# Attention and two gated layers on one core: batch 0's transposed q copied by either engine, its left-over tokens transposed after the first scores, another seed of the planner

## The chip, the cores and the metric

The kernel runs on one core of a Trainium2 chip. The metric is the device time of one launch in microseconds (us), and the time quoted for a kernel is the median of its runs. The core's engines are TensorE (PE in the profile; PEld is its loading of weights), VectorE (DVE), ScalarE (ACT), GpSimd (POOL) and SyncE (SP), which here issues nearly all DMAs. Each engine works through its own list of instructions in order.

## The reference

Three layers follow each other, all in float32 (the scales of the inputs are left out).

```python
# attention over 32 memory slots: q, k, v are (4, 8, 576, 64), phi is (4, 8, 576, 32)
a = softmax(phi, axis=2)                       # over the 576 tokens
k_m, v_m = einsum('bhsm,bhsd->bhmd', a, k), einsum('bhsm,bhsd->bhmd', a, v)
attn = softmax(q @ k_m.T / 8, axis=-1)         # over the 32 slots
x = (attn @ v_m) as (2304, 512)
# first layer, 512 -> 1536 -> 512
xn = x / sqrt(mean(x * x) + 1e-6) * rms_g
x = (silu(xn @ w_gate) * (xn @ w_val)) @ w_out
# second layer, 512 -> 2048 -> 512
h = x @ w_in
g = where(h >= 1, h, where(h <= -1, 0, (h + 1) ** 2 / 4))
out = g @ w_out2
```

## The kernel before, in words

**The order is made by a planner.** The program is written as some hundred streams (Python generators). A stream yields the engine that its next step needs with the planner's guess of its duration (`yield "A", 0.6` is 0.6 us of ScalarE), then emits the step. The class `Agenda` holds the streams and picks at each turn the one that can start first, by priority where they tie. A yield such as `"VAhi", (0.45, 0.68)` lets the planner pick the engine (V for VectorE, A for ScalarE, G for GpSimd) that would be done first. `"flag"` waits until another stream has called `mark`, `"take"` and `"give"` count buffers. The order in which steps are emitted is the order in which every engine runs them. Line 54 holds `SEED, WOBBLE`: each planned duration is multiplied by a random factor within 3% of 1 (in `run`), drawn from that seed, so another seed gives another order of the whole program, and with it other choices of engine.

**Attention, per batch b.** `soft` takes the maximum of phi over the tokens (folds on line 516, TensorE steps of lines 534 and 545), subtracts it (line 553, VectorE) and exponentiates (line 521, ScalarE). The tile is phi0 to phi3. `memory` sums phi-weighted k and v on TensorE (line 606, tile kvps), adds the sums of the weights (line 625, which wait for tile s1, made on GpSimd for batches 1 to 3), divides on VectorE (lines 635 to 652, tiles r, kd, vs), transposes (lines 660 and 663, tile kT) and copies the memory keys to kmT (line 669, ScalarE). `spread_v` (line 687) makes vbd from vs on VectorE or GpSimd.

**Scores.** `pair` handles 256 tokens of one batch; there are two pairs for each batch, and two further ones for the left-over 64 tokens of two batches each. A pair transposes its q on TensorE in two halves (line 772, tile qps), and `copy_q` copies each half to qT with ScalarE (line 758). Then `scores` multiplies qT with kmT (line 723, tile sc). The softmax over slots follows: maximum (line 791), difference (797), exponential (806), sum (810), its inverse (812, 813) and the product with it (815), then a transpose (823), its copy (827), the product with vbd (844, tile xp), squares (835), the scaling on GpSimd (856 to 862), a last transpose (870, tile ATp) and the split into a high and a low part (881, 883: Ah and Al, for batches 2 and 3 in the tile late).

**Left-over q.** `rest_q(b)` transposes the left-over 64 tokens of q (line 708, tile qrps) once q of the batch is there, and copies them with ScalarE (line 712, tile qr). Its score step is on line 734. The tile q0 is free for another batch when all three of its readers (two pairs and `rest_q`) have emitted their transposes.

**Weights and the first layer.** While this goes on, the weights of the first layer are loaded as raw 64-bit words (line 326) and turned into floats (`convert`, lines 339 to 362, on three engines; line 346 is the GpSimd form of the step on line 344). `vw` multiplies them with the batch's memory values on TensorE (line 934, tile vwps), ScalarE and VectorE split the result (952, 954). `gv` makes gate and value (line 984, tiles gps and vps; gps0_0_1 is batch 0, chunk 0, second half); `gate`, `splits` and `out1` (line 1079, tile ops) follow, then the second layer (`quads` line 1423, `outs` line 1546).

**Heat.** Until kmT3 is there, `heat` fills gaps that the planner sees on TensorE with matmuls of zeros (line 586).

Of the kernel before, what the change touches and what calls it, by code (L numbers as in the profile page):

```python
# [13 lines left out]
AF = mybir.ActivationFunctionType  # L14
# [36 lines left out]
OVER = {"V": 0.085, "A": 0.1}  # L51
FETCH = (256, 63, 80.0, 6.1, 3.6, 80)
TICK = 3.413
SEED, WOBBLE = 4, 0.06
WARM = 1.38
P_SOFT, P_PAIR, P_CONV, P_VW, P_GV, P_OUT1, P_W2, P_F2 = 0, 100, 800, 102, 850, 900, 3000, 4000
P_W = 4004
# [172 lines left out]
def tile_attn_moe(tc, q, k, v, phi, w_gate, w_val, w_out1, rms_g, w_in2, w_out2, out):  # L230
# [10 lines left out]
    nc = tc.nc  # L241
# [37 lines left out]
    def bank(tag, name):  # L279

        early = BANKS.get(tag + "0") if "attention" not in agenda.flags else None
        z = yield "pick", early or BANKS[tag]
        return psum.tile([P, 512], F32, tag=f"b{z}", name=name), ("bank", z)
# [23 lines left out]
    add, mark = agenda.add, agenda.set  # L307
# [388 lines left out]
    def used_q(b):  # L696
        q_left[b] -= 1
        if q_left[b] == 0:
            yield "give", "q"

    def rest_q(b):
        yield "flag", ("q", b)
        yield "take", "qr"
        qp, q_bank = yield from bank("q", f"qrps{b}")
        yield "P8", 0.43
        qv = qp.rearrange("p (c n) -> p c n", c=4)[0:D]
        for c in range(4):
            nc.tensor.transpose(qv[:, c, :], q_t[b][:, c, J - 1, :], ident)
        yield from used_q(b)
        yield "A", 0.6  # L710
        t = qr_t[b] = st.tile([P, 4, P], F32, tag="qr", name=f"qr{b}", bufs=BUFS["qr"])[0:D]
        nc.scalar.activation(out=t, in_=qv, func=AF.Copy)
        yield "give", q_bank
        mark(("qr", b))

    def scores(pr, qT, scv, w):
        if pr[0] < B:
            for i in range(2):
                yield "Ps32", 0.5
                for c in range(2 * i, 2 * i + 2):  # L720
                    for g in range(2):
                        for k in range(2):
                            nc.tensor.matmul(  # L723
                                out=scv[HP * k : HP * k + HP, 4 * g + c], lhsT=qT[:, c, g, k],
                                rhs=kmT_t[pr[0]][:, 4 * g + c].rearrange("p j m -> p (j m)"),
                                start=True, stop=True, skip_group_check=True,
                            )
            yield "give", "qT"
            return
        yield "Ps64", 1.0  # L730
        for c in range(4):
            for g in range(2):
                for k, bb in enumerate(RESTS[pr[1]]):
                    nc.tensor.matmul(
                        out=scv[HP * k : HP * k + HP, 4 * g + c], lhsT=qr_t[bb][:, c, HP * g : HP * g + HP],
                        rhs=kmT_t[bb][0:D, 4 * g + c, 0], start=True, stop=True, skip_group_check=True,
                    )
        for _ in RESTS[pr[1]]:
            yield "give", "qr"
# [6 lines left out]
    def pair(n):  # L746
        pr = pairs[n]
        b, jj = pr
# [5 lines left out]
        qT = None  # L754

        def copy_q(i, qv, q_bank):
            yield "A", 0.6
            nc.scalar.activation(out=qT[:, :, :, i], in_=qv, func=AF.Copy)
            yield "give", q_bank
            mark(("qT", pr, i))  # L760

        if b < B:
            yield "flag", ("q", b)
            yield "take", "qT"
            qT = st.tile([P, 4, 2, 2, HP], F32, tag="qT", name=f"qT_{name}", bufs=BUFS["qT"])
            for i in range(2):
                qp, q_bank = yield from bank("q", f"qps_{name}_{i}")
                yield "P8", 0.43
                qv = qp.rearrange("p (c g n) -> p c g n", c=4, g=2)
                j = 4 * jj + 2 * i  # L770
                for c in range(4):
                    nc.tensor.transpose(  # L772
                        qv[:, c].rearrange("p g n -> p (g n)"), q_t[b][:, c, j : j + 2].rearrange("p j d -> p (j d)"), ident
                    )
                add(pri, copy_q(i, qv, q_bank))
            yield from used_q(b)
        else:
            for bb, _ in per_batch(pr):
                yield "flag", ("qr", bb)
        for bb, _ in per_batch(pr):  # L780
            yield "flag", ("km", bb)
        if b < B:
            for i in range(2):
                yield "flag", ("qT", pr, i)
        sc, s_bank = yield from bank("s", f"sc_{name}")
        sc = sc[:, 0 : NB * M]
        yield from scores(pr, qT, sc.rearrange("p (h n) -> p h n", h=H), w)
        yield "take", "e"
        yield "V", 0.11 + 0.56 * w
        mx = st.tile([P, H, I], F32, tag="mx", name=f"mx_{name}", bufs=BUFS["e"])  # L790
        nc.vector.tensor_reduce(
            out=mx.rearrange("p h j -> p (h j)"), in_=sc.rearrange("p (n m) -> p n m", m=M),
# [5 lines left out]
            out=et, in0=sc.rearrange("p (h j m) -> p j h m", h=H, j=I),  # L798
# [15 lines left out]
        eng = yield "GVe", (0.2 + 0.9 * w, 0.12 + 0.57 * w)  # L814
        (nc.vector if eng == "V" else nc.gpsimd).tensor_tensor(
            out=e, in0=e, in1=sm.unsqueeze(2).to_broadcast([P, NB, M]), op=ALU.mult
# [22 lines left out]
        for i in range(I):  # L839
            xp, x_bank = yield from bank("x", f"xp_{name}_{i}")  # L840
            yield f"P{8 * len(per_batch(pr))}", 0.86
            for g in range(2):
                for bb, rows in per_batch(pr):
                    nc.tensor.matmul(  # L844
                        out=xp[rows, 256 * g : 256 * g + 256],
# [6 lines left out]
        for i in range(I):  # L852
# [4 lines left out]
            out=y, in0=ss, scalar1=1.0 / DM, scalar2=1e-6, op0=ALU.mult, op1=ALU.add  # L857
# [5 lines left out]
            out=ev, in0=ev, in1=y.unsqueeze(2).to_broadcast([P, I, HM]), op=ALU.mult  # L863
# [345 lines left out]
    for n in range(len(pairs)):  # L1209
        add(P_PAIR + n, pair(n))  # L1210
        if pairs[n][0] < B and pairs[n][1] == 1:
            add(P_PAIR + n, rest_q(pairs[n][0]))
# [456 lines left out]
```

## Time and profile before

| what | us |
|---|---|
| median of the runs shown (3) | 773.75 |
| the runs | 773.43, 773.75, 1912.09 |
| the profiled execution, its own time | 773.81 |
| its span | 772.0 |
| TensorE busy in it, zeros included | 759.0 |
| VectorE, ScalarE, GpSimd busy in it | 621.6, 462.7, 61.1 |

The span runs from the first to the last instruction of the profiled execution, and 1.8 us of its time lie outside the span. The prediction works in times of the span's start (so 21.00 us is 21.00 us into the span). A row of the timeline is: start, duration, engine, line, operation, what it writes and reads, how many such instructions are merged in the row, and in brackets how long the engine sat idle before it and what ended that. Matmuls are pipelined, so that the durations in a row with x1 overlap those of its neighbours. TensorE runs a plain f32 multiplication as two passes, which is why the trace counts 32 where the order prints x16.

### The profile page before, as it was taken

The numbers are of one execution on the slowest core, as the hardware profiler recorded it, in microseconds if no ns is written. First come the engines' busy times: TensorE is split into PE (matmuls) and PEld (weight loads), VectorE is DVE, ScalarE is ACT, GpSimd is POOL, SyncE is SP. The second block draws the span as 40 slices with busy tenths as digits, with TensorE's granted clock in tenths as the row PEclk, the third lists the DMA queues.
The fourth block names the chain that finished last, engine by engine and source line by source line (L and its number), as shares of the span: only waits on it lengthen the run. The fifth ranks groups of instructions, "written<-read, shape, count | busy, mean of one in ns | idle before, by whom it ended". The sixth has DMA issues, their size and how long they took to land.

```text
span 772.0 us, 17234 instructions
## 1 busy us (share of the span) xinstructions
PE 759.0 (98%) x6383; PEld 700.6 (91%) x6383; DVE 621.6 (81%) x1257; ACT 462.7 (60%) x959; POOL 61.1 (8%) x84
## 2 busy tenths in 40 slices
PE   8899999999999999999999999999999999999997
PEld 4678888889999888988899999999999999999997
DVE  5798889998877787756789889997789895589963
ACT  2688887755556555645566656564467463565552
POOL 1556610000001000000000000000000000000000
PEclk9999999999999999999999999999999999999999
DMA  9995535788779775599647999779888878757866
GB/s 343 377 385 160 199 111 188 258 275 270 253 237 305 251 248 187 205 324 324 208 168 219 326 305 305 252 249 318 293 251 262 296 241 258 254 182 251 270 217 209
DMA packets 113371, 197.49 MB, mean 256 GB/s; under 512 B 10372, under 2 KB 41096, under 8 KB 113288
## 3 DMA queue, kind: packets, MB, share of 16 engines
q1 hardware_dynamic: 112368, 194.88, 75.4%
q10 hardware_dynamic: 920, 1.51, 0.5%
q8 instruction: 51, 0.84, 0.4%
q14 instruction: 32, 0.26, 0.1%
HBM read 151.26 MB, written 45.09 MB: 254 GB/s over the span
## 4 chain that ended last, share of the span: by engine, by line
PE 92%; DVE 3%; DMA 2%; ACT 1%; issue 1%; ACTq 0%; SPq 0%; DVEq 0%
PE ops L1079 18%; PE acc_b L1546 17%; PE qb L1423 12%; PE gps L984 10%; PE vps L984 10%; PE qc L1423 6%; PE acc_c L1546 6%; PE qa L1423 3%; PE vwps L934 3%; PE xp L844 2%; DMA kv<-in_k_dram 1%; PE kvps L606 1%; PE sc L723 1%; PE qps L772 1%; DMA x1B<-x_d 1%
## 5 line engine op out<-in xcount | busy, mean ns | idle before, releaser
L1079 PE MATMUL ops<-ab,wo1h 128*128 128x512 f32 (+1 forms) x480 | 137.2, 371 | 0.5 <-ACT xs L1093 0.5
L1423 PE MATMUL qb<-xop,wr 128*128 128x384 f32 x576 | 111.7, 337 | 0.0
L1423 PEld LDWEIGHTS qb<-xop,wr 128*128 128x128 f32 x576 | 100.3, 187 | 0.9 <-DVE xop L1298 0.5
L1079 PEld LDWEIGHTS ops<-ab,wo1h 128*128 128x128 f32 x480 | 84.7, 189 | 15.8 <-issue 2.9
L1079 PE MATMUL ops<-ab,wo1l 128*128 128x512 f32 (+1 forms) x240 | 88.4, 368 | 0.0
L1546 PE MATMUL acc_b<-wor,gg_A 128*128 128x256 f32 x648 | 80.8, 280 | 1.0 <-ACT gg_A L1494 0.8
L1546 PEld LDWEIGHTS acc_b<-wor,gg_A 128*128 128x128 f32 x648 | 79.3, 188 | 1.3 <-ACT gg_A L1494 1.0
L1385 ACT ACTIVATE u<-qb 128x384 f32<-128x384 f32 x72 | 35.2, 489 | 49.7 <-PE qb L1423 49.1
L1423 PE MATMUL qc<-xop,wr 128*128 128x384 f32 x288 | 58.3, 337 | 0.0
L1546 PE MATMUL acc_c<-wor,gg_S 128*128 128x256 f32 x432 | 53.0, 279 | 0.0
L1079 PEld LDWEIGHTS ops<-ab,wo1l 128*128 128x128 f32 x240 | 45.2, 188 | 7.9
L1546 PEld LDWEIGHTS acc_c<-wor,gg_S 128*128 128x128 f32 x432 | 52.2, 188 | 0.0
L1546 PE MATMUL acc_b<-wor,gg_S 128*128 128x256 f32 x432 | 51.7, 279 | 0.0
L1546 PEld LDWEIGHTS acc_b<-wor,gg_S 128*128 128x128 f32 x432 | 51.3, 188 | 0.0
L1423 PEld LDWEIGHTS qc<-xop,wr 128*128 128x128 f32 x288 | 50.9, 187 | 0.0
L344 ACT ACTIVATE raw<-raw 128x512 uint32<-128x512 uint32 x68 | 45.3, 673 | 0.0
L1016 ACT ACTIVATE kvth<-gps 128x64 f32<-128x64 f32 (+2 forms) x101 | 28.9, 305 | 18.8 <-PE gps L984 18.5
L984 PE MATMUL gps<-late,vwh 128*128 128x288 f32 x192 | 39.6, 294 | 0.0
L984 PE MATMUL vps<-late,vwh 128*128 128x288 f32 x192 | 39.6, 294 | 0.0
L1050 ACT ACTIVATE ab<-kvth 128x512 fp32r<-128x512 f32 (+1 forms) x40 | 22.7, 566 | 26.1 <-PE ops L1079 26.1
L954 DVE TENSOR_TENSOR vwl<-vwps,vwh 128x512 fp32r<-128x512 f32 x48 | 32.3, 685 | 7.2 <-ACT vwh L952 6.9
L1494 ACT ACTIVATE gg_S<-gs 128x384 fp32r<-128x384 f32 x52 | 26.8, 522 | 17.5 <-PE acc_b L1546 8.5
(188 smaller groups left out, 1730.1 us busy)
## 6 DMA issues: line engine op xcount, KB each, us to landing
wr<-win_d SPq DMA_DIRECT2D x168, 256.0 KB, 4.0
wor<-wout_d SPq DMA_DIRECT2D x168, 256.0 KB, 3.3
raw<-in_moe_w_out_dram SPq DMA_DIRECT2D x28, 512.0 KB, 4.9
win_d<-wins SPq DMA_DIRECT2D x56, 256.0 KB, 2.8
wout_d<-wouts SPq DMA_DIRECT2D x56, 256.0 KB, 2.9
raw<-in_moe_w_in_dram SPq DMA_DIRECT2D x16, 512.0 KB, 4.9
raw<-in_moe_w_gate_dram SPq DMA_DIRECT2D x12, 512.0 KB, 4.8
raw<-in_moe_w_val_dram SPq DMA_DIRECT2D x12, 512.0 KB, 5.7
```

The lines of the kernel that those rows point to most:

```text
L344: nc.scalar.activation(out=low, in_=low, func=AF.Copy, scale=LOW_SCALE, bias=LOW_BIAS)
L844: nc.tensor.matmul(out=xp[rows, 256 * g : 256 * g + 256], lhsT=aT[:, i, g, rows], rhs=vbd_t[bb][:, g].rearrange("p h d -> p (h d)"), start ...
L934: nc.tensor.matmul(out=vps[g][0][32 * c : 32 * c + 32, 2 * P * x : 2 * P * x + 2 * P], lhsT=vT[n // NF1 * 2 + x][hs, c, :], rhs=t[hs, c].r ...
L954: nc.vector.tensor_tensor(out=lv, in0=vps[g][0], in1=hv.bitcast(F32), op=ALU.subtract)
L984: nc.tensor.matmul(out=p[:, 0:HB], lhsT=wt[:, g, i, :], rhs=at[b][:, g, c], start=(g == 0 and y == 0), stop=(g == 1 and y == 2),)
L1016: nc.scalar.activation(out=t, in_=g[:, c], func=AF.Silu)
L1050: nc.scalar.activation(out=ah, in_=src, func=AF.Copy)
L1079: nc.tensor.matmul(out=p[:, 0:n], lhsT=wt[:, fc, d], rhs=at, start=(fc == 0 and x == 0), stop=(fc == NF1 - 1 and x == 2),)
L1385: nc.scalar.activation(out=u, in_=src, func=AF.Copy)
L1423: nc.tensor.matmul(out=bank, lhsT=wt[:, kc, :], rhs=xt[:, kc, :], start=(start and kc == 0 and i == 0), stop=(kc == 1 and i == 2), skip_gr ...
L1494: nc.scalar.activation(out=t[:, 0], in_=src, func=AF.Copy)
L1546: nc.tensor.matmul(out=acc[x + "001"[t]][:, t % 2], lhsT=g[:, gi, P * t : P * t + P], rhs=w[:, wi], start=((o, t) in FIRST and q == 0 and ...
```

## The change

Three edits. The copies of batch 0's transposed q may go to ScalarE or to VectorE, as the planner picks (0.60 and 0.62 us in its book); those of the other batches stay on ScalarE. The left-over tokens of q of batch 0 are transposed only once the scores of the first pair (0, 0) have been emitted. The seed is 17 instead of 4.

```diff
-SEED, WOBBLE = 4, 0.06
+SEED, WOBBLE = 17, 0.06
...
     def rest_q(b):
+        if b == 0:
+            yield "flag", ("sc", (0, 0))
         yield "flag", ("q", b)
         yield "take", "qr"
...
         def copy_q(i, qv, q_bank):
-            yield "A", 0.6
-            nc.scalar.activation(out=qT[:, :, :, i], in_=qv, func=AF.Copy)
+            if b == 0:
+                eng = yield "AVq", (0.6, 0.62)
+            else:
+                yield "A", 0.6
+                eng = "A"
+            if eng == "A":
+                nc.scalar.activation(out=qT[:, :, :, i], in_=qv, func=AF.Copy)
+            else:
+                nc.vector.tensor_copy(out=qT[:, :, :, i], in_=qv)
             yield "give", q_bank
             mark(("qT", pr, i))
...
         yield from scores(pr, qT, sc.rearrange("p (h n) -> p h n", h=H), w)
+        mark(("sc", pr))
         yield "take", "e"
```

**TensorE at the first scores.** qps_0_1_1 is the last of batch 0's four transposed pieces of q, qrps0 its left-over tokens, sc_0_0 and sc_0_1 the scores of its two pairs. Before:

```order
L772 MATMUL qps_0_1_0_291<-ident_85,q0_176 128x128 x4
L772 MATMUL qps_0_1_1_324<-ident_85,q0_176 128x128 x4
L708 MATMUL qrps0_292<-ident_85,q0_176 64x128 x4
L723 MATMUL sc_0_0_338<-kmT0_104,qT_0_0_288 64x64 x16
L586 LDWEIGHTS zeros_115
L586 MATMUL heat_123<-zeros_115 128x512
```

The same place of the changed kernel:

```order
L781 MATMUL qps_0_1_0_292<-ident_85,q0_177 128x128 x4
L781 MATMUL qps_0_1_1_323<-ident_85,q0_177 128x128 x4
L725 MATMUL sc_0_0_333<-kmT0_104,qT_0_0_289 64x64 x16
L725 MATMUL sc_0_1_353<-kmT0_104,qT_0_1_291 64x64 x16
L710 MATMUL qrps0_362<-ident_85,q0_177 64x128 x4
L586 LDWEIGHTS zeros_115
L586 MATMUL heat_123<-zeros_115 128x512
```

The left-over tokens moved behind both scores. The zeros between the scores (four matmuls before, then one behind sc_0_1) now stand together behind the left-over tokens, five of them, ahead of kvps1.

**ScalarE at the copies of q.** qT_0_1 is the transposed q of pair (0, 1), phi1 the exponential of batch 1. Before:

```order
L758 ACTIVATE qT_0_0_288<-qps_0_0_1_305 128x8x64
L758 ACTIVATE qT_0_1_290<-qps_0_1_0_291 128x8x64
L521 ACTIVATE phi1_165<-phi1_165 128x1152
L712 ACTIVATE qr0_357<-qrps0_292 64x512
L758 ACTIVATE qT_0_1_290<-qps_0_1_1_324 128x8x64
L806 ACTIVATE e_0_0_370<-e_0_0_370 128x512
```

Now:

```order
L765 ACTIVATE qT_0_0_289<-qps_0_0_1_304 128x8x64
L765 ACTIVATE qT_0_1_291<-qps_0_1_0_292 128x8x64
L521 ACTIVATE phi1_166<-phi1_166 128x1152
L714 ACTIVATE qr0_388<-qrps0_362 64x512
L816 ACTIVATE e_0_0_379<-e_0_0_379 128x512
L816 ACTIVATE e_0_1_394<-e_0_1_394 128x512
```

One of batch 0's four copies left ScalarE, the second half of qT_0_1. On VectorE it stands between vT0 and the first maximum, as the only new row there (`L767 COPY`).

**TensorE at batch 3's memory.** kT3 holds the memory keys and values of batch 3 transposed, s13 the sums of its weights, vwps1 chunk 1 of the weights times the memory values, gps0_0_1 a gate product. Before:

```order
L625 MATMUL kvps3_1_1017<-consts_67,s13_1014 128x1
L772 MATMUL qps_3_0_1_1147<-ident_85,q3_955 128x128 x4
L772 MATMUL qps_3_1_1_1149<-ident_85,q3_955 128x128 x4
L708 MATMUL qrps3_1095<-ident_85,q3_955 64x128 x4
L586 LDWEIGHTS zeros_115
L586 MATMUL heat_1190<-zeros_115 128x512
L660 MATMUL kT3_1189<-ident_85,kd3_1163 128x128 x2
L663 MATMUL kT3_1189<-ident_85,vs3_1164 128x128
L870 MATMUL ATp_1_1_1177<-ident_85,e_1_1_816 128x128 x4
```

Now, with the rows just ahead of kT3:

```order
L833 MATMUL aTp_2_1_1213<-ident_85,e_2_1_1098 128x128 x4
L994 MATMUL gps0_0_1_1222<-Ah0_94,vwh0_827 128x288
L994 MATMUL gps0_0_1_1222<-Al0_96,vwh0_827 128x288
L994 MATMUL gps0_0_1_1222<-Ah0_94,vwl0_828 128x288
L944 MATMUL vwps1_0_1235<-w1_329,vT0_90 32x256 x4
L944 MATMUL vwps1_1_1236<-w1_329,vT0_90 32x256 x4
L944 MATMUL vwps1_0_1235<-w1_329,vT1_91 32x256 x4
L944 MATMUL vwps1_1_1236<-w1_329,vT1_91 32x256 x4
L660 MATMUL kT3_1261<-ident_85,kd3_1182 128x128 x2
L663 MATMUL kT3_1261<-ident_85,vs3_1183 128x128
L854 MATMUL xp_2_1_0_1264<-vbd2_110,aT_2_1_1239 128x256 x2
```

kT3 moved behind a gate product, both transposes of batch 2's weights and all of vwps1, which stood some 100 rows earlier before. Between the step with s13 and kT3 there are now six matmuls of zeros where one stood. gps0_0_0 and vps0_0_0, the first gate and value products, moved ahead of the whole of kvps3 (they stood behind kT3). Over the whole program TensorE issues 54 matmuls of zeros instead of 46; all other matmuls are the same in number. In the first 92 us GpSimd gets one vbd step more (line 687), one step of line 346 that it did not have, and one step of line 362 less.

## Rows read from the trace of the kernel before

**Rows 1.** Five stretches: length, then busy PE, PEld, DVE, ACT, POOL; clock, DMA, GB/s.

```profile
0.00:11.48 11.48, 8.74 (x36) 3.57 (x37) 4.80 (x12) 2.63 (x3) 3.13 (x18) 1.00 0.86 308
11.48:22.56 11.08, 10.74 (x251) 7.96 (x252) 7.04 (x20) 4.96 (x9) 3.06 (x4) 1.00 1.06 392
22.56:57.43 34.87, 32.18 (x639) 25.42 (x639) 31.05 (x72) 26.73 (x54) 19.25 (x23) 1.00 1.06 381
57.43:92.00 34.57, 33.09 (x450) 27.71 (x450) 30.45 (x66) 30.07 (x71) 24.76 (x33) 1.00 0.48 158
92.00:772.00 680.00, 674.23 (x5010) 635.97 (x5008) 548.28 (x1091) 398.27 (x823) 10.91 (x8) 1.00 0.76 251
```

**Rows 2.** The same stretches, zeros (L586) alone: length, PE, PEld, clock, DMA, GB/s.

```profile
0.00:11.48 11.48, 8.26 (x30) 3.07 (x30) 1.00 0.86 308
11.48:22.56 11.08, 2.90 (x11) 0.91 (x11) 1.00 1.06 392
22.56:57.43 34.87, 0.97 (x3) 0.35 (x3) 1.00 1.06 381
57.43:92.00 34.57, 0.76 (x2) 0.20 (x2) 1.00 0.48 158
```

**Rows 3.** Timeline, 17 to 23 us, the first scores.

```profile
17.05 1.53 PE L772 MATMUL qps<-ident,q 128*128 128x128 f32 x12
...
18.42 0.60 PE L708 MATMUL qrps<-ident,q 128*64 128x128 f32 x4
18.44 0.28 DVE L676 TENSOR_TENSOR vT<-kT,gT 128x128 f32<-128x128 f32 x1
18.72 1.17 ACT L521 ACTIVATE phi<-phi 128x1152 f32<-128x1152 f32 x1
...
18.95 1.15 PE L723 MATMUL sc<-kmT,qT 128*64 128x64 f32 x32
19.77 0.58 ACT L712 ACTIVATE qr<-qrps 64x512 f32<-64x512 f32 x1
...
20.03 1.04 PE L586 MATMUL heat<-zeros 128*128 128x512 bf16 x4
20.15 0.69 DVE L791 TENSOR_REDUCE mx<-sc 128x16 f32<-128x512 f32 x1 [1.42 <-PE sc L723]
20.25 0.58 ACT L758 ACTIVATE qT<-qps 128x512 f32<-128x512 f32 x1
...
21.00 1.15 PE L723 MATMUL sc<-kmT,qT 128*64 128x64 f32 x32
...
22.59 1.11 PE L606 MATMUL kvps<-kv,phi 64*32 64x128 f32 x61
```

**Rows 4.** Timeline, 31 to 67 us: q of batch 2, the memory of batch 3.

```profile
31.02 2.12 SPq L493 DMA_DIRECT2D q<-in_q_dram  x1
...
61.87 0.39 PE L625 MATMUL kvps<-consts,s 64*128 64x1 f32 x4
...
64.21 0.53 PE L660 MATMUL kT<-ident,kd 128*128 128x128 f32 x2 [0.28 <-DVE vs L652]
...
66.89 0.69 PE L723 MATMUL sc<-kmT,qT 128*64 128x64 f32 x16
```

**Rows 5.** One line's instructions from 30 to 92 us, durations in ns: min/median/max.

```profile
L350 DVE SCALAR_TENSOR_TENSOR w<-w,raw x12: 628/812/1576, 36.9 to 85.5; 128x512 uint32<-128x512 uint32 x12
```

**Rows 6.** Waits of PE's matmuls, whole span: us in total, times, longest.

```profile
PE kvps L606 <- issue: 2.4, 2, 1.6
...
PE acc_b L1546 <- ACT gg_A L1494: 0.8, 1, 0.8
PE vps L984 <- ACT kvth L1016: 0.7, 1, 0.7
PE xp L844 <- ACT aT L827: 0.5, 1, 0.5
PE ops L1079 <- ACT xs L1093: 0.5, 1, 0.5
```

## Prediction

> **What bounds the kernel now.** I read the stretches first [rows 1]. The reader is to compare TensorE's busy time with the length. From 92 us to the end it works 674.23 of 680.00 us at the granted clock of 1.00, so nothing but its own matmuls sets the pace there: 5.8 us are all that the later 88% of the span could ever give back. VectorE (548) and ScalarE (398) have room in it. So the time is decided by how late TensorE reaches its dense stretch, and that lies in the first 92 us.
>
> There the busy time misleads, because part of it is multiplication of zeros, which the next view counts by itself [rows 2]. Length less useful work gives what each stretch loses: 11.48 - (8.74 - 8.26) = 11.0 us before the first k lands; 11.08 - (10.74 - 2.90) = 3.2; 34.87 - (32.18 - 0.97) = 3.7; 34.57 - (33.09 - 0.76) = 2.2. The first 11 us are a wait for a load that the change does not touch. What can be won ahead of 92 us is 3.2 + 3.7 + 2.2 = 9.1 us. The other engines show why it is lost: from 22.56 to 57.43 us VectorE is busy 31.05 of 34.87 us, and the DMA share is 1.06; from 57.43 to 92 us VectorE and ScalarE are busy some 30 of 34.6 us each. The head is a chain through nearly full engines.
>
> One distinction carries the sum. A zero matmul is emitted into TensorE's list and has to be executed, needed or not. Real idle is only length less busy: 0.34 us in the stretch to 22.56, 2.69 to 57.43 and 1.48 to 92. Of that 4.2 us of the last two, 2.4 is TensorE waiting for "issue", nothing that the profile shows [rows 6]. About 1.8 us are waits for another engine, such as 0.7 for ScalarE at vps and 0.5 at xp [rows 6].
>
> **The change part by part.** *The first scores.* Now the second pair's scores start at 21.00, because ScalarE copies the last piece of qT only at 20.25, behind phi's exponential (18.72) and the copy of the left-over q (19.77) [rows 3]. With that copy on VectorE, which is done with vT at 18.72 and then idles 1.42 us until 20.15 [rows 3], it can be there at 18.72 plus its own time. The trace of before has no such copy; the nearest rows are 0.58 us for the same copy on ScalarE and 0.69 us for a VectorE instruction reading the scores, as many elements [rows 3]. I take 0.69, the same engine, hence 19.41. The first scores no longer stand behind qrps (0.5 us of TensorE) and can start when the transposes end, 17.05 + 1.53 = 18.6 instead of 18.95. They take about 1.1 us, so the second ones start at 19.7, after the copy, 1.3 us earlier than 21.00. What hides the copy is VectorE's idle time; without that cover the first maximum would come up to 0.69 us later.
>
> What is late next? Behind the scores come qrps (0.5) and five zeros instead of four and one. Four zeros took 1.04 us [rows 3], 0.26 each, so 1.3 us: 19.7 + 1.1 + 0.5 + 1.3 = 22.6, where kvps of batch 1 starts now, 22.59. The zeros give the 1.3 us back, as they must, since TensorE's list is as long as before and its idle time in that stretch was only 0.34 us. Bounds -0.34 and, if the zeros end late, +0.3; I take -0.2, nearer to the row of idle time. VectorE does get its second maximum and difference some 1.5 us sooner, which counts below as fewer waits.
>
> *The left-over tokens.* They moved behind both scores, so q0 is released some 2 us later than 18.42 + 0.6 = 19.0. The load that needs its place, q of batch 2, is issued at 31.02 [rows 4], since SP's list has four loads of raw weights ahead of it: 10 us of cover, cost nothing; without cover it would cost what the release is late, 2 us. The copy to qr has its reader 20 us later. Nothing else queues behind the new wait: the stream only emits later.
>
> *The other seed, up to 92 us.* The matmuls on TensorE are the same, except for 54 zeros instead of 46. Eight at 0.26 us are +2.1 us; at 0.22, if 0.16 of the four's 1.04 us were the last one's tail, +1.8. I take 2.1. Against it stand the waits that the new order can remove. gps0_0_0 and vps0_0_0 moved ahead of batch 3's kvps, and gps0_0_1 and vwps1 ahead of kT3, so TensorE has work where it waited for other engines. That is at most the 1.8 us above, at worst nothing, or below nothing if new waits come. I take two thirds, -1.2, because most of the waits that rows 6 name there are short ones behind ScalarE.
>
> *After 92 us.* The order of TensorE is nearly the same, with gates a little further ahead and other interleavings late. Bounds: -1.3, if its two longest waits went (0.8 and 0.5 [rows 6]), and +6, if seven or eight of the longest size were added; I take 0.
>
> Sum: -0.2 + 2.1 - 1.2 + 0 = +0.7 us on the profiled execution's own 773.81 us (772.0 of span and 1.8 around it), hence 774.5 us. The median of the runs shown is 773.75, so nothing is to be added for that.
>
> **A rule of the skill.** In the head one VectorE line, L350, takes 628 ns at best and 1576 ns at worst with the same shape [rows 5]. The Trainium skill (page "SBUF — State Buffer", section "Who interferes with whom") says that VectorE and GpSimd share a pair of ports under an exclusive lock, and that a two-input operation on tiles in SBUF is held up by GpSimd's reads. The spread of that row agrees. The new order gives GpSimd one vbd step and one step of line 346 more and one of line 362 less in the head. By the row alone a further clash costs VectorE 1.576 - 0.628 = 0.95 us.
>
> **The rivals.** *A gain after all.* The issue waits of 2.4 us may go too, as they hang on where TensorE's list happens to stand. Then the sum is 0.7 - 2.4 = -1.7: 772.1 us. For it: the early work on VectorE. Against it: the waits are for no engine that the change relieves.
>
> *Batch 3 comes late, slower.* Now kT3 starts at 64.21, 2.3 us behind the step with the weights' sums at 61.87, and the scores of batch 3 at 66.89 [rows 4]. In the new order kT3 waits in TensorE's list behind vwps1, which needs weight chunk 1 complete, and behind batch 2's transposes, with six zeros on the way. If kT3 moves by the five zeros more (1.3 us) and by GpSimd and VectorE being late with these inputs, batch 3's softmax finds ScalarE and VectorE (30 of 34.6 us busy) in the middle of weight conversion. It costs when TensorE has no gate work left ahead of batch 3's transposes. The price is then the 2.2 us that this stretch loses now, a second time, with the waits not removed: 0.7 + 1.2 + 2.2 = +4.1, or 777.9 us. Against it: gates of batches 0 and 1 are plentiful by then.
>
> *A late clash of another order.* Four waits of 0.8 us in the second layer make +3.2 on the sum: 777.7 us. Against it: the longest there today are the 0.8 and the 0.5 [rows 6].
>
> *The shared ports.* Two clashes of 0.95 us that TensorE feels make 774.5 + 1.9 = 776.4 us; VectorE's 10% of idle time speaks against it.
>
> *The change does not do what it says.* The order shows only one of four copies on VectorE; if it lands no earlier, -0.2 goes: 774.7 us, inside the forecast.
>
> **How the numbers follow.** Forecast (773.3 to 775.7) 0.43; gain 0.22; batch 3 late 0.16; late clash 0.13; ports 0.06. The gain case reaches to 770 with the late waits gone, the slow ones to 780 where two fall together; that leaves out about 1 in 10 and is the range. A measurement of this kernel tells about 2% from no change, 15.5 us. All that could be won is 9.1 + 5.8 us, below that, so faster gets 0.01. Slower than 789 needs three of the slow cases at once: 0.02. The rest, 0.97, is the same within 2%.
>
> **What would show it.** In the profile after: sc_0_1 near 19.7 us and kvps of batch 1 still near 22.6; a VectorE copy of 0.6 to 0.7 us at 18.7; q of batch 2 issued near 31; zeros' busy time up by about 2 us between 57 and 72 us; idle TensorE time from 22.56 to 92 us near 3 us; kT3 near 70 us without a long wait ahead of aTp of batch 3; TensorE idle after 92 us near 6 us. The forecast is wrong if the zeros' stretch was already idle time that vanishes, or if a wait over 2 us stands in the dense stretch.

## The result, and the profile after

The changed kernel takes 778.12 us (median of 4 runs, 777.27 to 779.52), the kernel before 773.59 beside it: a ratio of 1.0060, 95% interval 1.0048 to 1.0072. One of the kernel before's four runs, 1912.09 us, was slow and the ratio leaves it out. The change costs 4.5 us (3.7 to 5.6), well inside 2%. The forecast was 774.5 with a range of 770 to 780. The profiled execution has 778.37 us of its own and a span of 776.6.

The five stretches of [rows 1], in the changed kernel (columns as there):

```profile
0.00:11.48 11.48, 9.37 (x43) 3.82 (x47) 4.25 (x10) 2.63 (x3) 3.12 (x18) 1.00 0.86 307
11.48:22.56 11.08, 10.45 (x251) 7.87 (x252) 9.25 (x26) 4.61 (x9) 3.08 (x4) 1.00 1.06 393
22.56:57.43 34.87, 32.30 (x615) 26.16 (x616) 28.22 (x65) 26.19 (x56) 18.82 (x25) 1.00 1.04 371
57.43:92.00 34.57, 31.80 (x441) 25.21 (x440) 29.58 (x64) 26.11 (x61) 22.15 (x28) 1.00 0.42 138
92.00:776.60 684.60, 677.39 (x5050) 638.98 (x5050) 551.85 (x1093) 404.09 (x836) 17.12 (x14) 1.00 0.76 251
```

The zeros alone, as in [rows 2]:

```profile
0.00:11.48 11.48, 8.85 (x30) 3.27 (x30) 1.00 0.86 307
11.48:22.56 11.08, 2.71 (x11) 1.00 (x11) 1.00 1.06 393
22.56:57.43 34.87, 1.57 (x5) 0.49 (x5) 1.00 1.04 371
57.43:92.00 34.57, 2.39 (x8) 0.70 (x8) 1.00 0.42 138
```

From 22.56 to 92 us TensorE now stands idle for 2.57 + 2.77 = 5.3 us, against 2.69 + 1.48 = 4.2 before, and multiplies zeros for 3.96 us, against 1.73. The waits of its matmuls over the whole span, to be read against [rows 6], name new places (aTp is the transpose ahead of the product xp, kvth the function of a gate product on ScalarE, acc_b and gg_A belong to the second layer):

```profile
PE acc_b L1556 <- ACT gg_A L1504: 1.6, 2, 0.8
PE kvps L606 <- issue: 1.6, 2, 0.9
PE aTp L833 <- POOL e L825: 1.3, 1, 1.3
PE vwps L944 <- ACT kvth L1026: 1.3, 1, 1.3
...
PE xp L854 <- ACT aT L837: 1.0, 1, 1.0
```

The first scores came as forecast. In the timeline from 17 to 23 us, against [rows 3], the scores of both pairs are one row, the copy stands on VectorE, and batch 1's memory starts at 22.59 as before. The bracket says why it can't start sooner: it waits for v.

```profile
18.46 2.09 PE L725 MATMUL sc<-kmT,qT 128*64 128x64 f32 x64
18.59 0.68 DVE L767 COPY qT<-qps 128x512 f32<-128x512 f32 x1
...
20.94 1.24 PE L586 MATMUL heat<-zeros 128*128 128x512 bf16 x5
...
22.59 1.11 PE L606 MATMUL kvps<-kv,phi 64*32 64x128 f32 x61 [0.41 <-DMA kv<-in_v_dram]
```

Where the time goes is seen with a cut at 64 us. First the kernel before, then the changed one; columns as in [rows 1]:

```profile
0.00:64.00 64.00, 58.15 (x1105) 42.15 (x1105) 47.35 (x115) 39.61 (x79) 31.69 (x53) 1.00 0.95 342
64.00:72.00 8.00, 7.79 (x84) 6.55 (x85) 7.78 (x18) 7.96 (x20) 2.60 (x5) 1.00 0.34 101
72.00:84.00 12.00, 11.50 (x110) 10.12 (x110) 11.06 (x23) 10.62 (x24) 10.64 (x12) 1.00 0.60 198
84.00:96.00 12.00, 11.31 (x110) 9.84 (x109) 10.03 (x23) 9.47 (x25) 5.28 (x8) 1.00 0.71 260
```

```profile
0.00:64.00 64.00, 58.69 (x1082) 43.53 (x1083) 47.77 (x108) 37.59 (x76) 30.15 (x53) 1.00 0.91 326
64.00:72.00 8.00, 7.03 (x66) 5.21 (x72) 6.59 (x17) 6.25 (x15) 6.58 (x8) 1.00 0.18 70
72.00:84.00 12.00, 11.27 (x168) 9.41 (x152) 9.89 (x25) 9.14 (x22) 5.96 (x8) 1.00 0.70 218
84.00:96.00 12.00, 9.80 (x83) 7.24 (x84) 8.82 (x17) 9.40 (x23) 7.25 (x11) 1.00 0.39 133
96.00:776.60 680.60, 674.51 (x5013) 636.65 (x5011) 550.08 (x1090) 401.25 (x830) 14.34 (x10) 1.00 0.77 252
```

Length less useful work (busy less zeros, which are 12.51, 0, 0.38 and 0 us before and 13.13, 2.01, 0.38 and 0 now) is lost time: 18.4 us before and now up to 64 us; then 0.2 against 3.0 up to 72, 0.9 against 1.1 up to 84, and 0.7 against 2.2 up to 96. From 96 us to the end it is 6.1 now and was 5.8 before. So nearly all the loss, 2.8 + 1.5 us, lies between 64 and 96 us, in batch 3 and what follows it:

```profile
64.87 0.39 PE L625 MATMUL kvps<-consts,s 64*128 64x1 f32 x4
65.19 0.82 PE L586 MATMUL heat<-zeros 128*128 128x512 bf16 x3
66.06 0.81 PE L586 MATMUL heat<-zeros 128*128 128x512 bf16 x3
66.71 0.60 PE L833 MATMUL aTp<-ident,e 128*128 128x128 f32 x4
68.28 1.99 PE L854 MATMUL xp<-vbd,aT 128*128 128x256 f32 x8 [0.97 <-ACT aT L837]
...
71.44 1.09 PE L944 MATMUL vwps<-w,vT 64*32 64x256 f32 x32
72.47 0.44 PE L660 MATMUL kT<-ident,kd 128*128 128x128 f32 x2
```

The step with batch 3's sums starts 3.0 us later than in [rows 4], kT3 8.3 us later, and chunk 1's product (vwps) stands just ahead of it. After that the gates are short. The matmuls of gate and value alone from 84 to 96 us, in the kernel before:

```profile
84.00:96.00 12.00, 8.71 (x57) 7.67 (x57) 1.00 0.71 260
```

and in the changed one:

```profile
84.00:96.00 12.00, 2.61 (x17) 2.41 (x18) 1.00 0.39 133
```

It had run 12 of them by 64 us, when the kernel before had run none, but of the chunks' products only one (32 matmuls of the line), where the kernel before had two (64): there was less to go on with.

### The profile page after: what moved, and what is told of

Read it like the earlier page. It is cut to its first block, busy times and chain, and to the rows that moved or that the text cites. A ratio compares the mean times of both kernels' runs of the same rounds, so it can differ in the third digit from the quotient of the medians.

```text
span 776.6 us, 17258 instructions
## 1 busy us (share of the span) xinstructions
PE 761.3 (98%) x6391; PEld 702.0 (90%) x6391; DVE 623.1 (80%) x1254; ACT 463.6 (60%) x962; POOL 64.3 (8%) x87
## 4 chain that ended last, share of the span: by engine, by line
PE 93%; DMA 3%; ACT 1%; issue 1%; DVE 1%; SPq 1%; POOL 0%; ACTq 0%; POOLq 0%
PE ops L1089 19%; PE acc_b L1556 16%; PE qb L1433 13%; PE gps L994 10%; PE vps L994 10%; PE qc L1433 7%; PE acc_c L1556 6%; PE qa L1433 3%; PE vwps L944 3%; PE xp L854 2%; DMA kv<-in_v_dram 2%; PE kvps L606 1%; PE sc L725 1%; DMA x1B<-x_d 1%; PE qps L781 1%
## 5 line engine op out<-in xcount | busy, mean ns | idle before, releaser
L344 ACT ACTIVATE raw<-raw 128x512 uint32<-128x512 uint32 x65 | 43.5, 675 | 0.6 <-DMA raw<-in_moe_w_in_dram 0.4
L962 ACT ACTIVATE vwh<-vwps 128x512 fp32r<-128x512 f32 x48 | 27.8, 596 | 17.2 <-PE vwps L944 17.2
```

Source lines behind the costliest of these rows:

```text
L344: nc.scalar.activation(out=low, in_=low, func=AF.Copy, scale=LOW_SCALE, bias=LOW_BIAS)
L962: nc.scalar.activation(out=hv, in_=vps[g][0], func=AF.Copy)
```

## Experiments

Three theories stood at the start: A, seed 17's order is slow because batch 3 and chunk 1 come late in it; B, the two edits cost the time; C, every order that the planner draws is a lottery ticket of its own. The plainest test, both edits with the old seed 4, has no time: the order drawn there deadlocks. Each kernel was timed beside the kernel before on the same chip (773.89 to 774.05 in each set).

**The seed alone.** The kernel before, with `SEED = 17`.

> Seed 17 without the two edits. kT3 is row 183 and stands 11 rows behind vwps1, as in the changed kernel (4 rows there); 44 zeros instead of 54. Theory A: 776.5 to 778.5, with kT3 after 70 us. Rival B: 773.6 within 1. Rival C: anything from 772 to 778, with no tie to where kT3 stands.

778.61 us, ratio 1.0058 (1.0045 to 1.0071). Without either edit the seed costs the same 4.6 us: against B. It loses only in part in the same place: from 64 to 72 us 2.0 us (the changed kernel 3.0), but from 96 us on 8.5 us, where the kernel before loses 5.8. The longest of its waits after 300 us are

```profile
PE acc_b L1546 <- DVE gg_A L1496: 1.1, 1, 1.1
PE acc_b L1546 <- ACT gg_A L1494: 0.8, 1, 0.8
PE qa L1423 <- ACT xop L1296: 0.6, 1, 0.6
```

of which [rows 6] have the 0.8 alone.

**Each edit alone, with the old seed.** The changed kernel with `SEED = 4`, once without the flag in `rest_q`, once with `copy_q` as before.

> The copy on either engine alone, with seed 4 (the copy lands on VectorE; the left-over tokens stand ahead of the scores, as before). The draws after it fall differently, so the order further on is a new one: chunk 1's product 43 rows ahead of kT3, 46 zeros. Theory A (a seed-17 order is slow because batch 3's memory and chunk 1 come late in it): 774 within 1. Rival B (the edits cost it): 777 or more. Rival C (every order is a draw, spread over 772 to 779): anywhere in it.

> The left-over tokens behind the first scores alone, with seed 4 (all copies stay on ScalarE). Chunk 1's product stands 58 rows ahead of kT3, 46 zeros. Theory A: 774 within 1. Rival B: 777 or more. Rival C: anywhere from 772 to 779.

781.8 us (1.0102, 1.0089 to 1.0115) and 781.87 us (1.0097, 1.0083 to 1.0112): the slowest of all, and above the 772 to 779 that C had named, though chunk 1's product stands 43 and 58 rows ahead of kT3. So an order can be slow without kT3 close behind vwps1; what that place does in seed 17's order these runs don't tell. Part of the 8 us is the clock: all eight executions have a mean granted clock of 0.995 to 0.998, the kernel before 0.999 or 1.000. In the profiles it is 0.57 from 49 to 53 us and 0.53 from 85 to 92 us; length times missing clock makes at most 1.7 and 3.3 us (estimates). By themselves these two runs would speak for B; the last run below tells.

**A third seed.** Both edits, `SEED = 6`.

> Both edits with a third seed, 6: 45 zeros, chunk 1's product 33 rows ahead of kT3, kT3 at row 166. Theory A: 774 within 1.5. Rival B: 777 or more. Rival C: anywhere from 772 to 779.

778.34 us (1.0058, 1.0046 to 1.0070), here too with a lower clock, 0.993 to 0.998 in all five executions (0.66 from 43 to 48 us in the profile, by the same estimate at most 1.7 us). With this, five orders other than that of before have been timed: 778.1, 778.3, 778.6, 781.8 and 781.9.

**The late zeros.** The next experiments keep the changed kernel's order on every engine, so that nothing is drawn anew. Here the last eight zeros are planned but not issued.

```diff
-        last = t = None
+        last, t, n = None, None, 0
...
-            nc.tensor.matmul(
+            (n := n + 1) <= 46 and nc.tensor.matmul(
```

> The changed kernel in the same order, without the 47th to 54th matmul of zeros (57 to 92 us; the other 46 stay). If zeros cost what they take, as the prediction's +2.1 has it: 778.1 - 2.4 = 775.7, the 2.39 us that these eight were busy. If they only fill waits for VectorE and GpSimd, 778.1 within 0.4, and the idle time of TensorE from 57.43 to 92 us is up by some 2 us. If the clock falls without them, slower, and the granted clock of that stretch shows it.

779.25 us (1.0070, 1.0056 to 1.0083), no gain. In its timeline the zeros turned into named waits:

```profile
66.63 0.66 PE L833 MATMUL aTp<-ident,e 128*128 128x128 f32 x4 [0.75 <-POOL e L825]
68.30 1.99 PE L854 MATMUL xp<-vbd,aT 128*128 128x256 f32 x8 [1.01 <-ACT aT L837]
...
71.46 1.09 PE L944 MATMUL vwps<-w,vT 64*32 64x256 f32 x32
```

These starts agree with those of the changed kernel, shown above, within 0.1 us. These zeros cost nothing; they show where the planner saw TensorE wait. The higher median goes with a lower clock, of which the last section tells: the two executions at 1.000 took 777.65 and 778.18 us.

**The copy's engine.** `copy_q` issues on ScalarE what the planner gave to VectorE.

> The changed kernel in the same order on every engine, but the one copy of q on VectorE issued on ScalarE instead (there it stands ahead of batch 1's exponential). If the copy's cover is as the prediction says (kvps of batch 1 waits for v until 22.59 us): 778.1 within 0.4. If what follows the first scores hangs on it, the exponential of batch 1 is 0.6 us later and the time 778.7 or more. If VectorE's copy was what made the change slow: 776 to 777.5.

779.08 us (1.0065, 1.0052 to 1.0079). Its profile keeps the changed kernel's pace up to 93 us (the product of chunk 2 starts at 93.33 against 93.12) and then runs at a lower clock, of which the last section tells. Its three executions at 0.999 or 1.000 took 777.6 to 778.1 us, those of the changed kernel 777.3 to 778.4: the copy's engine makes no difference that these runs can show.

**GpSimd relieved.** In the same order, four products (line 825, `b in (2, 3)`) and the last step of chunk 1's first half go to VectorE, so that the step on ScalarE that fed it is no longer needed; the eight zeros are left out.

> The changed kernel in its order, with GpSimd relieved between 65 and 86 us: the products of batches 2 and 3 (four instructions of 1.0 to 1.6 us) and the last step of chunk 1's first half (1.77 us) are done by VectorE at the place where they are issued, and the eight late zeros are left out. If GpSimd, which works without a gap from 57 to 70 us, is what TensorE waits for there: the 2.4 us of zeros and the waits of 1.3 and 1.0 go, less 0.7 for VectorE, so 775 to 776.5. If VectorE (29.6 of 34.6 us busy there) only takes the delay over: 777.5 or more.

780.02 us (1.0073, 1.0055 to 1.0091; single runs 777.02 to 781.68). No gain in the median; the two executions with a mean clock of 1.000, 777.02 and 777.34, compare with 777.27 and 778.37 of the changed kernel. By these few, relieving GpSimd is worth some 0.6 us, not the 1.5 to 3 of the theory, which speaks against GpSimd alone as the brake.

**The two longest waits, one by one.** A Silu of one column behind the last exponential brings ScalarE's table load forward; batch 3's two products move to VectorE; both; and the first edit on the kernel before.

```diff
...
-        nexp[0] -= 1
+        nexp[0] -= 1; nexp[0] or nc.scalar.activation(out=warm, in_=half, func=AF.Silu)
...
-        (nc.vector if eng == "V" else nc.gpsimd).tensor_tensor(
+        (nc.vector if eng == "V" or b == 3 else nc.gpsimd).tensor_tensor(
```

> The changed kernel in its order, with one more ScalarE instruction: a Silu of one column right behind the last exponential, so that the table for Silu is loaded at 81 to 83 us instead of at 91.30, where chunk 2's product waits 1.26 us behind it. Theory D (the 4 us come from the waits between 76 and 96 us, each felt in full at the end): 1.0 to 1.3 less than the changed kernel's 778.1, so 776.8 to 777.1, and fewer executions with a lower clock. Rival E (the waits take each other's place; the head is bound by the total of VectorE's and ScalarE's work): 777.7 or more, with the wait come back in another place before 100 us.

777.69 us (1.0053, 1.0041 to 1.0066). The load moved, and the wait ahead of chunk 2's product is gone:

```profile
81.29 1.28 ACT L817 ACT_TABLE_LOAD   x1
...
84.77 0.66 PE L833 MATMUL aTp<-ident,e 128*128 128x128 f32 x4 [1.30 <-POOL e L825]
...
91.81 1.54 PE L944 MATMUL vwps<-w,vT 64*32 64x256 f32 x32
93.28 0.66 PE L880 MATMUL ATp<-ident,e 128*128 128x128 f32 x4
```

The changed kernel has the aTp at 84.93 and this ATp at 94.12: ahead by 0.16, then by 0.84, so 0.7 of the 1.26 us are won. The median is 0.4 us lower, which the intervals don't tell from nothing, and lies between the two theories.

> The changed kernel in its order, but batch 3's two products with the inverse sums are issued on VectorE instead of GpSimd, which started the second at 83.29 us and let TensorE wait 1.31 us at 84.93. Theory D: that wait is gone or under 0.4: 776.8 to 777.3. Rival E: VectorE's 1.4 us more come back as another wait: 777.7 or more.

778.86 us (1.0063, 1.0051 to 1.0076). The wait fell from 1.31 to 0.74, behind VectorE now. The aTp behind it starts 0.36 us sooner, and this lead is kept up to chunk 2's product (92.73 against 93.12), whose own wait stayed at 1.27. Then the granted clock is 0.57 from 94 to 98 us, and the next chunk starts at 102.88 against 101.72. So the median, which shows no gain, holds a loss by the clock, and doesn't decide between the theories.

```profile
84.57 0.63 PE L833 MATMUL aTp<-ident,e 128*128 128x128 f32 x4 [0.74 <-DVE e L825]
```

> Both of the last two edits on the changed kernel. Theory D: the two waits are independent, 778.1 - 1.26 - 1.0 = 775.8, within 0.5. Rival E: 777 or more.

777.58 us (1.0050, 1.0037 to 1.0062): not the 775.8 of theory D. The two executions at 1.000 took 777.28 and 777.58 us, so the clock is not what hides it.

> The kernel before, in its order, with the Silu of one column behind its last exponential (79.74 us), so that the table is loaded there and not at 85.91 us, where TensorE waits 0.69 us at 87.67. Theory D: 0.4 to 0.7 faster, 773.2 to 773.5, which would beat both kernels. Rival E: the same within 0.2, or slower, as ScalarE (30.1 of 34.6 us busy there) delays a copy that TensorE needs.

774.4 us (1.0007, 0.9998 to 1.0017): no gain. The 0.69 us of the table load went, and its waits between 76 and 96 us are now

```profile
PE xp L844 <- ACT aT L827: 0.9, 2, 0.5
PE ATp L870 <- POOL w L362: 0.4, 1, 0.4
```

against 0.5 at xp and 0.7 at vps in [rows 6]: 1.3 us after 1.2. Here one wait took the other's place.

**Both edits in the old order.** To part the edits from the redrawing, they were written by hand into the kernel before: the copy is issued on VectorE right behind its transposes, and qrps0 is held until the scores of pair (0, 0) have been issued. Apart from these two, every engine's list is that of before.

```diff
...
-        for c in range(4):
-            nc.tensor.transpose(qv[:, c, :], q_t[b][:, c, J - 1, :], ident)
+        held.append(lambda: [nc.tensor.transpose(qv[:, c, :], q_t[b][:, c, J - 1, :], ident) for c in range(4)])
+        b and held.pop()()
...
-            return
+            return held and held.pop()()
...
-            nc.scalar.activation(out=qT[:, :, :, i], in_=qv, func=AF.Copy)
+            (pr, i) == ((0, 1), 1) or nc.scalar.activation(out=qT[:, :, :, i], in_=qv, func=AF.Copy)
...
-                add(pri, copy_q(i, qv, q_bank))
+                add(pri, copy_q(i, qv, q_bank)); (pr, i) == ((0, 1), 1) and nc.vector.tensor_copy(out=qT[:, :, :, i], in_=qv)
```

> The kernel before in its own order on every engine, with both edits made by hand: the last of the four copies of batch 0's transposed q stands on VectorE ahead of vT0, and the left-over tokens are transposed behind the scores of pair (0, 0); nothing else moves. Theory O (the edits are worth nothing either way, because kvps of batch 1 waits for v until 22.59 us; the 4.5 us are the new order's): 773.9 within 0.4. Rival B (the edits cost it): 776 or more. Rival G (the edits gain, and the new order hides it): 773.2 or less.

774.01 us against 774.03: ratio 1.0001 (0.9992 to 1.0010). The copy stands at 18.64, but the four zeros still stand ahead of the second pair's scores, which start at 21.04, as before (21.00). Batch 1's memory waits for v:

```profile
18.54 1.15 PE L723 MATMUL sc<-kmT,qT 128*64 128x64 f32 x32
18.64 0.69 DVE L775 COPY qT<-qps 128x512 f32<-128x512 f32 x1
...
20.08 1.03 PE L586 MATMUL heat<-zeros 128*128 128x512 bf16 x4
...
21.04 1.15 PE L723 MATMUL sc<-kmT,qT 128*64 128x64 f32 x32
...
23.04 1.11 PE L606 MATMUL kvps<-kv,phi 64*32 64x128 f32 x61 [0.53 <-DMA kv<-in_v_dram]
```

In the old order the two moves cost nothing and gain nothing. B falls, and with it the reading of the two runs with seed 4: they were slow because a single edit drew them another order. What second scores some 1.5 us sooner, as in the changed kernel, would be worth in the old order is not shown, since the zeros hold them back there. C is left: every other order timed was slower. No version tried beats the kernel before; what makes its order better than the five others was not isolated. Whether seed 4 had once been picked for its time is not on record; that all five others are slower would fit it.

## Why the prediction was right or wrong

The time lies inside the range of 770 to 780 us, but not inside the forecast's own 773.3 to 775.7: the room left for the slow rivals holds it. The sum missed by 3.6 us.

- *The first scores, -0.2.* Right in every place: the scores of pair (0, 1) are the second half of the row 18.46 to 20.55 (forecast 19.7), the copy takes 0.68 us (taken: 0.69), kvps of batch 1 starts at 22.59. Nothing was gained by then; in the old order the moves measure 0.0, with the second scores no earlier. The prediction put the stop down to the zeros in TensorE's list; the bracket names v, which lands no sooner.
- *The left-over tokens, 0.* Right: q of batch 2 is issued at 31.00 us, before at 31.02 [rows 4].
- *Eight zeros, +2.1.* Mis-sized. They were busy for 15.52 us in all, 2.6 more than the 12.89 of [rows 2], but leaving the late eight out gave nothing back. A zero that stands in a wait costs 0; the term should have been the wait beneath it.
- *Waits removed, -1.2.* This is the step that failed: "I take two thirds, -1.2, because most of the waits that rows 6 name there are short ones behind ScalarE." The old short waits did change, but new ones came, 1.31 us for GpSimd, 1.26 for the table load, 0.97 for ScalarE's copy, and a stretch with zeros up to 67 us. With the zeros counted as the waits that they are, the stretches from 64 to 96 us lost 4.5 us more (0.2 + 0.9 + 0.7 against 3.0 + 1.1 + 2.2). That is nearly the whole result.
- *After 92 us, 0.* 1.4 us too low as it was put: 7.2 us idle from 92 us on, against 5.8. Of this 1.1 is the table load's wait, which began before 92 us and ends at 93.12; from 96 us on, 6.1 against 5.8, the term is right.
- *The rivals.* "Batch 3 comes late, slower" (777.9, chance 0.16) is what the profile shows, nearly at its price. The prediction held against it that "gates of batches 0 and 1 are plentiful by then": from 84 to 96 us TensorE ran 57 gate products before and 17 now. Its size was a fit of two numbers rather than a mechanism, and the cause it gave, vwps1 ahead of kT3, is no rule: the two runs with seed 4 are slow without it. Which of the late things (chunk 1, the sums, kT3) was first, the runs don't settle: relieving single waits gave 0.7 us at best. "A gain after all": the issue waits at kvps fell from 2.4 to 1.6 us, but the one at the scores of left-over tokens grew from 0.2 to 1.0. "A late clash": the second wait of 0.8 at acc_b came, but from 96 us on only 0.3 us more is lost. "The shared ports": the row of [rows 5] is busy 11.1 us in the changed kernel (11 instructions, 651 to 1799 ns), before 11.6 us (12), so no more clashes show there. "The change does not do what it says" was wrong: the copy moved and landed in time.

The forecast weighed an order like an edit, row by row. It should have asked how far redrawing any part of this order moves the time: here by 4 to 8 us (in three of the five orders partly by the clock), each time to the slow side, while the edits move it by nothing in the old order.

## What to carry to other kernels

Where a planner with random factors sets the order, time an edit first in the old order, by hand, and only then in a new one; otherwise the draw is measured, not the edit. See in its timeline that it does there what it was meant to do. Count filler work as the wait that it covers: add it to the idle time, stretch by stretch, and never add it as a cost of its own. And a kernel whose engines are all nearly full for 30 us can give little back when one wait is taken away: here 0.7 of 1.26 us in one order, nothing of 0.69 us in the other.

## What the runs showed of the hardware

**Behind a wait the clock can fall and cost about as much again.** In its profile, the kernel with the copy on ScalarE waits 1.25 us before the product at 93.33, as the changed kernel does before its 93.12. Then it runs at the lower clock (0.50, the level of 1.2 GHz, for the whole of 95 and 96 us; columns as in [rows 1]):

```profile
92.00:94.00 2.00, 0.75 (x25) 0.44 (x24) 0.52 (x2) 1.26 (x3) 1.92 (x5) 1.00 0.03 12
94.00:98.00 4.00, 4.00 (x25) 3.68 (x18) 2.27 (x4) 3.11 (x6) 0.98 (x1) 0.57 0.01 4
98.00:102.00 4.00, 4.00 (x33) 4.00 (x33) 2.80 (x8) 2.30 (x7) 0.00 (x0) 1.00 0.20 79
```

Its next chunk starts at 103.50, in the changed kernel at 101.72. It was 0.2 us behind and is now 1.8: 1.6 us went to the clock. The changed kernel had the same wait and kept 2.4 GHz in its profile, so such a wait does not always bring the fall. With batch 3's products on VectorE the clock fell at the same place, from 94 to 98 us. With both of the last two edits on the changed kernel it fell behind a wait of 0.98 us at 43.56 (0.57 from 44 to 48 us); the changed kernel waits 0.98 us at 43.78 and keeps its clock. The kernel with the left-over edit alone had the longest, 2.63 us ahead of a gate product at 85.73, with the clock at half all the way from 86 to 91 us:

```profile
83.00:86.00 3.00, 0.37 (x2) 0.27 (x2) 2.97 (x7) 1.24 (x4) 2.52 (x2) 0.78 0.00 0
86.00:91.00 5.00, 5.00 (x17) 4.45 (x18) 3.29 (x11) 1.81 (x5) 0.83 (x2) 0.50 0.67 246
```

The clock also goes with how far executions of one kernel lie apart. The six of the kernel without the late zeros, by mean granted clock:

```
clock  1.000   1.000   0.998   0.997   0.996   0.993
us     777.65  778.18  778.95  779.56  780.65  781.78
```

All runs of the kernel before beside them have 0.999 or 1.000 and lie within 1.3 us. Whether the late zeros guard the clock stays open: without them four of six executions were at 0.998 or less; with them one of four, three of six with the copy on ScalarE, and seven of fifteen in the three kernels with one or both of the two longest waits changed.
